# Matmul fillers of 384 columns, fillers between attention and experts, and another order of PSUM banks

## The chip, the cores and the metric

The kernel runs on one core of one Trainium2 chip. A core has TensorE (PE: matmuls, with its weight loads listed apart as PEld), VectorE (DVE), ScalarE (ACT), GpSimd (POOL), and SyncE (SP), which here only issues DMAs. The engines run their own instruction streams and meet at semaphores. PE writes into PSUM[...]; DVE and ACT read PSUM, POOL doesn't touch it here. The metric is device time in microseconds, the median over several executions. One further execution is recorded by the hardware profiler; its rows are what is quoted below.

## The reference: softcapped attention, then soft mixture of experts

Eight batches, twelve heads, 448 tokens, 64 per head. The attention's output, laid out as x of 3584 tokens by 768, is the input of a soft mixture of 8 experts with 4 slots each (32 slots), hidden size 1024.

```python
# attention, per batch and head
scores = cap * np.tanh(scale * (q @ k.T) / cap)          # cap = 30
attn = np.exp(scores - scores.max(-1)); attn /= attn.sum(-1)
x = attn @ v                                             # -> [3584, 768]
# experts
logits = x @ phi                                         # [3584, 32]
d = softmax(logits, axis=0); slot_input = d.T @ x        # [32, 768]
for e in range(8):                                       # 4 slots of each expert
    slot_out[e] = np.maximum(slot_input[e] @ w1[e], 0) @ w2[e]
out = softmax(logits, axis=1) @ slot_out                 # [3584, 768]
```

The slots' sums run over all tokens of all batches. So the experts can't begin before the last token of attention has its logits, and no output can be stored before the experts are done.

## The kernel before: tiling, stages and the order of work

**Attention.** Heads are taken in pairs. A tile is 64 keys of both heads of a pair (two 64x64 corners of the array) against 448 queries. Six tiles make a chunk; there are 56 chunks. For each, `qk_chunk` (L295) writes the scores into PSUM, `tanh_chunk` (L304) and `exp_part` (L308) turn them into bf16 weights on ACT; for some tiles DVE works out the exp by a polynomial (L335 to L340). `pv_mms` (L358) multiplies by the values with a column of ones beside them, `norm` (L365, L368) divides by the row sums into xq, `x_transp` (L406, L411, L417) transposes, `logits` multiplies by phi (L423, L427), and `slot_sums` adds e^logits times x into the slots (L494, L500). The order on each engine is written by hand: `at(j, slot, f, ...)` puts a function into one of the places of chunk j, and `run(j, slot)` plays it there. Nothing is rescheduled, so an instruction that waits holds up all that are queued behind it on its engine.

**Fillers.** `busy(n)` (L612) issues n matmuls of ones by ones, 128 columns each, whose result nobody reads. `spare(n)` gives them a fresh PSUM tile "junk" in the bank that the attention's output uses (pool psV, one buffer); `fill(n)` writes 57 columns beside the output instead. They are placed by the list FILL (10 and 12 in chunk 6 of each batch), by a few calls for the first two chunks, and in the chunks NCH-6, NCH-4 and NCH-2, the last of which has 12. Before the first data arrive, `busy(4)` and `busy(28)` run on a boot tile. The tile of ones is 128x128 and is set by DVE (L77).

**Between attention and experts.** After the last chunk, seven banks of PSUM (b0 to b6) are dealt out by `bank()` from a list, `turns`; when the list is empty it goes on with (6, 3, 0, 1, 2). In order they hold the output of the last pairs (pvm, pvl), the last logits (lpl), the last slot sums (slpl, two banks with 96 columns in use of 512), one half of the last transposes (xpl), the sums of the softmax (zps), then the experts' tiles. The steps on PE are: `x_transp(last - 1)`; `x_last(0)` transposes the first part of the last pair, ACT copies; `z_last(bl - 1)` sums e for the batch before the last; `phi_last(last - 1, ...)`; `x_last(1)`, copied by DVE; `phi_last(last, ...)` for the first two groups of tokens, then `e_last(0)` on ACT; the remaining groups after DVE's copy, then `e_last(1)`; `slot_mms` (L494, L500); DVE adds them to slT (L759); `z_last(bl)`. Then `layer1` (L794): six steps for each of four halves, in every step four matmuls of 512 columns side by side, one per expert, in a quarter of the array's columns each.

**Experts and output.** `relu` on ACT and DVE, `h_transp`, then `layer2` (L827) into two banks so_ps, first for output columns 0 to 383, then for 384 to 767. The first so_ps is copied to so[0] (L878, L879), and while the second half of layer 2 runs, tiles of the output's first half are made by `half_tile` (L858, L863: a matmul by so, a scaling on ACT or DVE, a store from SP). Twelve of these "stored tiles" are made, numbers 0 to 11; number 0 takes two banks, the others one each. The last loop then uses a new pool, `fin`, of three tiles of two banks each in the same memory. A new tile waits until those who used its banks are done. The loop makes first the missing halves of the twelve tiles, still by `half_tile`, then whole tiles (L910, L917, L919). SP issues all stores (L843, L860). The weights w1 and part of w2 come in during attention; the rest of w2 was converted to bf16 in DRAM (w2d) and is read back by SP as w2t from the end of attention on.

Of the kernel before, what the change touches and what calls it, by code (L numbers as in the profile page):

```python
# [9 lines left out]
F32 = mybir.dt.float32  # L10
BF16 = mybir.dt.bfloat16
# [6 lines left out]
P = 128  # L18
# [18 lines left out]
def kernel(  # L37
# [12 lines left out]
    B, H, _, _ = q.shape  # L50
# [3 lines left out]
    NS = moe_phi.shape[1]  # L54
    NJ = D // P
# [13 lines left out]
    pe, dve, act, pool, sp = nc.tensor, nc.vector, nc.scalar, nc.gpsimd, nc.sync  # L69

    consts = ctx.enter_context(tc.tile_pool(name="consts", bufs=1))
# [1 line left out]
    psT = ctx.enter_context(tc.tile_pool(name="psT", bufs=1, space=PSUM))  # L73


    ones = consts.tile([P, P], BF16, name="ones")
    dve.memset(ones, 1.0)  # L77
    ident = consts.tile([P, P], BF16, name="ident")
    make_identity(nc, ident)
# [3 lines left out]
    half1 = consts.tile([P, 1], BF16, name="half1")  # L83
    pool.memset(half1, 0.0)
    pool.memset(half1[0:HP, :], 1.0)
    phib = consts.tile([P, NJ, NS], BF16, name="phib")
    ET4 = consts.tile([P, B // 2 - 1, NT, 2, HP], BF16, name="ET4")
    winv = consts.tile([P, B // 2, NT], F32, name="winv")
# [51 lines left out]
    for nm in ("ex1", "ex2", "vb0", "ex3", "ex4", "ex0", "vb1"):  # L140
        home = exps if nm[0] == "e" else vb
# [4 lines left out]
    psV = attp.enter_context(tc.tile_pool(name="psV", bufs=1, space=PSUM))  # L146
# [65 lines left out]
    def first_pieces(h, jobs):  # L212

        for stage, nm, c0, c1, eng, bank, at0 in jobs:
            copy = act.copy if eng is act else dve.tensor_copy
            cols = slice(h * HP, h * HP + HP)
            if stage == "cast":
                copy(casts[nm, 0][:, c0:c1, cols],
                     raws[nm, 0][h][:, c0 * DH:c1 * DH].rearrange("p (c d) -> p c d", d=DH))
            elif stage == "turn":  # L220
                for c in range(c0, c1):
                    pe.transpose(bank[cols, at0 + c - c0, :], casts[nm, 0][:, c, cols], ident)
            else:
                copy(qkT[nm, 0][cols, c0:c1, :], bank[cols, at0:at0 + c1 - c0, :])
# [146 lines left out]
    def xq_tile(pr):  # L371
        Q, h = divmod(pr, 2)
        if h == 0:
            xq[Q] = xs.tile([P, 2, NT, DH], BF16, name="xq", tag="xq")
# [25 lines left out]
    def turn_x(ps, q0, pr, gs):  # L400

        Q, h = divmod(pr, 2)
        for g in gs:
            c0 = g * P - q0
            if g < NF:
                pe.transpose(ps[:, c0:c0 + P],  # L406
                             xq[Q][:, h, 2 * g:2 * g + 2, :].rearrange("p i d -> p (i d)"), ident)
                continue
            for n in range(2):
                r = slice(n * HP, n * HP + HP)  # L410
                pe.transpose(ps[r, c0:c0 + HP], xq[Q][r, h, NT - 1, :], ident[r, r])  # L411
# [8 lines left out]
    def phi_mms(dst, t, g, jt, first, last):  # L420

        if g < NF:
            pe.matmul(dst, t[:, g * P:(g + 1) * P], phib[:, jt, :], start=first, stop=last,  # L423
                      skip_group_check=True)
            return
        for n in range(2):
            pe.matmul(dst[n * HP:n * HP + HP], t[:, TAIL:S], phib[:, jt, :], start=first,  # L427
                      stop=last, skip_group_check=True)
# [22 lines left out]
    def e_rep(b):  # L451

        e4s[b] = consts.tile([P, NG, 4 * NS], BF16, name="e4", tag="e4", bufs=1)
        pool.tensor_copy(e4s[b].rearrange("p g (a s) -> p g a s", a=4),  # L454
                         es[b].unsqueeze(2).to_broadcast([P, NG, 4, NS]))
# [63 lines left out]
    def at(j, slot, f, *a):  # L519
        if j < 0:  # L520
            j, slot = 0, "b"
        aux.setdefault((j, slot), []).append((f, a))
# [3 lines left out]
        hpads.append(consts.tile([P, E, NFT, NS], BF16, name="hpad", tag="work", bufs=1))  # L526
        pool.memset(hpads[0], 0.0)

    def spare(n):

        busy(n, psV.tile([P, P], F32, name="junk", tag="pv"))

    FILL = ((3, "a", fill, 2), (4, "a", fill, 2), (5, "a", fill, 2), (6, "a", spare, 10), (6, "c", spare, 12), (7, "a", fill, 18), (8, "a", fill, 8), (9, "a", fill, 2))
    PER = 2 * NQB * NT // CH
    assert PER == 7 and NQB == 3
# [11 lines left out]
    for b in range(B):  # L547
        j, p = b * PER, 6 * b
# [10 lines left out]
        if b == 0:  # L559
            at(j + 1, "d", spare, 34)  # L560
            at(j + 2, "d", spare, 4)
# [20 lines left out]
    for n, job in enumerate(wjobs):  # L582
        at(1 + n * (NCH - 5) // len(wjobs), "b", *job)
    for j, slot, n in ((0, "a", 10), (0, "c", 10), (1, "b", 10), (1, "c", 8)):
        at(j, slot, spare, n)
    for j, slot, n in ((NCH - 6, "d", 8), (NCH - 4, "d", 8), (NCH - 2, "d", 12)):
        at(j, slot, spare, n)
    id32s = []
# [18 lines left out]
    junk = boots[0][:, 0, 0:P]  # L607

    def busy(n, home=None, by=None):
        by = ones if by is None else by  # L610
        for _ in range(n):
            pe.matmul(junk if home is None else home, by, by, start=True, stop=True)  # L612

    busy(4, by=nc.const_aps.tensor(1.0, [P, P], BF16))
    junk = boots[1][:, 0, 0:P]
    busy(28)
    first_half(0)
    qk_chunk(0)
# [46 lines left out]
    attp.close()  # L665
    mid = ExitStack()
    big = mid.enter_context(tc.tile_pool(name="big", bufs=1, space=PSUM, reuse_waits="tile"))
    turns = [0, 1, 2, 6, 3, 4, 5, 0, 6, 3, 0, 1, 2, 4, 5]

    def bank(shape, dt=F32, name="bank"):  # L670
        n = turns.pop(0)
        if not turns:
            turns.extend((6, 3, 0, 1, 2))
        return big.tile(shape, dt, name=name, tag=f"b{n}")

    pvs[last - 1] = bank([P, NT, W], name="pvm")
    lps = [bank([P, 2, NS], name="lpl") for _ in range(2)]
    pv2 = [bank([P, 4, W], name="pvl") for _ in range(2)]
    sl_ps = [bank([P, NJ // 2, NS], name="slpl") for _ in range(2)]
    xq_tile(last - 1)  # L680
    run(NCH - 1, "t0")
    CM = sum(place[last - 1, c] < NTILE - 2 * CH for c in range(NT))
# [7 lines left out]
    for s in range(2):  # L690
        pe.matmul(lps[s], id32s[0], lg[:, 2 * s:2 * s + 2, :], start=True, stop=False,
                  skip_group_check=True)
# [12 lines left out]
    def phi_last(pr, gs, done=False):  # L705
        for g in gs:
            phi_mms(lps[g // 2][:, g % 2, :], xTs[pr], g, pr % NJ, False, done)
# [21 lines left out]
    def z_last(b):  # L729
        for g in range(NG):  # L730
            for a in range(4):
                pe.matmul(zl[32 * a:32 * a + NS, :], es[b][:, g, :],
                          ones[:, 0:1] if g < NF else half1, start=(b < bl and g == 0),
                          stop=(b == bl and g == NG - 1), skip_group_check=True)

    def x_last(s, copy):
        q0, q1 = 2 * s * P, min(2 * s * P + 2 * P, S)
        turn_x(xpl[s], q0, last, halves[s])
        copy(xTs[last][:, q0:q1], xpl[s][:, 0:q1 - q0])

    def e_last(s):
        act.activation(el[:, 2 * s:2 * s + 2, :], lps[s], ACT.Exp)

    x_last(0, act.copy)
    z_last(bl - 1)
    phi_last(last - 1, (0, 1, 2))
    x_last(1, dve.tensor_copy)
    phi_last(last, (0, 1), True)
    e_last(0)
    phi_last(last, (2,))  # L750
    phi_last(last - 1, (NF,))
# [7 lines left out]
        dve.tensor_tensor(slT[:, js, :], sl_ps[s], slacc[:, js, :], op=ALU.add)  # L759
    e_rep(bl)  # L760
    z_last(bl)
    dve.tensor_tensor(zacc, zl, zacc, op=ALU.add)
    dve.reciprocal(rz, zacc)
    att.close()
# [131 lines left out]
    for n in range(B // 2 * NT):  # L896
# [12 lines left out]
        for half in range(2):  # L909
            pe.matmul(op[:, half, 0:HD], et_tile(bb, c), so[half],  # L910
                      start=True, stop=True)
# [47 lines left out]
```

## Time and profile before

| what | value |
|---|---|
| median of 4 executions | 303.35 us |
| the four | 303.18, 301.55, 303.59, 303.53 us |
| the profiled execution, its own time | 303.18 us |
| its span, first to last instruction | 301.4 us |
| PE busy, matmuls | 265.2 us (88%), 4687 |
| ACT busy | 268.0 us (89%) |
| DVE busy | 236.8 us (79%) |
| POOL busy | 136.7 us (45%) |
| matmuls of the fillers in junk (L612), 128 columns | 264, 18.9 us busy |
| first matmul of layer 1 | 259.23 us |
| first store issued | 270.76 us |
| last DVE work | about 292.3 us |
| mean granted clock of TensorE | 0.98 |

Busy time of PE counts overlapping matmuls once; a matmul's duration (0.22 us for 128 columns) includes its passage through the array, and in a row of them one starts every 0.056 us. "PEclk" is the share of TensorE's full clock that was granted. In rows of time, `[0.76 <-DVE obh L865]` means that the engine was idle for 0.76 us and that what ended it was DVE's instruction of line 865; "issue" means that the profile shows nothing that it waited for. A row with x3 merges three instructions: its time runs from the first's start to the last's end.

### The profile page before, as it was taken

To read this page: it belongs to the slowest core of one execution; us is meant where nothing else is said; L and a number is where in the kernel's file an instruction comes from. 1 tells how busy PE (TensorE), PEld (TensorE's weight loads), DVE (VectorE), ACT (ScalarE), POOL (GpSimd) and SP (SyncE) were. 2 spreads that over 40 slices of the span, in tenths; PEclk is the share of its full clock that TensorE was granted. 3 is DMA by queue.
4 is the path that set the end of the run, shared out by engine and by line. 5 is a ranking of instruction groups with operands and counts; after the bars stand their busy time and mean duration, and the time that the engine had idled before them with its cause. 6 is when DMAs were issued, how large, how long until landed. Compare 5 with 4: busy or idle time off the path is not lost.

```text
span 301.4 us, 10675 instructions
## 1 busy us (share of the span) xinstructions
PE 265.2 (88%) x4687; PEld 181.4 (60%) x4687; DVE 236.8 (79%) x511; ACT 268.0 (89%) x211; POOL 136.7 (45%) x178
## 2 busy tenths in 40 slices
PE   8898988998899989988999899899999999998830
PEld 6665656665666666666666566666666677542410
DVE  3728989898988999899879998999899973236850
ACT  3999999999999999999999999999999998136740
POOL 4493663485439534953394349443933232000000
PEclk9999999999999999999999999999999999799995
DMA  7999999699999999999899999999999649918997
GB/s 266 199 204 206 206 218 198 141 213 206 232 182 198 200 232 201 208 203 232 152 156 221 229 225 189 195 231 228 171 203 232 194 113 358 410 71 320 403 424 315
DMA packets 58061, 67.70 MB, mean 225 GB/s; under 512 B 3872, under 2 KB 54304, under 8 KB 58016
## 3 DMA queue, kind: packets, MB, share of 16 engines
q0 software_dynamic: 42448, 35.31, 75.8%
q1 hardware_dynamic: 15280, 31.50, 29.1%
q8 instruction: 36, 0.59, 0.7%
q10 hardware_dynamic: 288, 0.23, 0.2%
q14 instruction: 9, 0.07, 0.1%
HBM read 91.32 MB, written 18.87 MB: 366 GB/s over the span
## 4 chain that ended last, share of the span: by engine, by line
ACT 69%; PE 18%; issue 5%; DVE 4%; POOL 1%; DVEq 0%; ACTq 0%
ACT ex L304 37%; ACT ex L308 28%; PE pv L358 3%; PE hp L794 2%; PE so_ps L827 2%; PE sc L295 2%; PE op L910 2%; ACT E L448 1%; ACT ob L919 1%; PE boot L612 1%; PE op L863 1%; DVE xq L368 1%; PE pvl L358 1%; DVE obh L865 1%; POOL vbd L273 1%
## 5 line engine op out<-in xcount | busy, mean ns | idle before, releaser
L304 ACT ACTIVATE ex<-sc 128x1344 bf16<-128x1344 f32 (+1 forms) x113 | 164.3, 1726 | 1.4 <-PE sc L295 1.4
L308 ACT ACTIVATE ex<-ex 128x2240 bf16<-128x2240 bf16 (+4 forms) x58 | 147.1, 2573 | 0.1
L358 PE MATMUL pv<-vbd,ex 128*128 128x130 bf16 (+1 forms) x1610 | 94.4, 211 | 10.4 <-POOL vbd L273 5.4
L358 PEld LDWEIGHTS <-ex 128*128 128x128 bf16 (+1 forms) x1680 | 76.0, 101 | 31.1 <-issue 6.6
L295 PE MATMUL sc<-qT,kT 64*64 64x448 bf16 x672 | 68.8, 359 | 4.7 <-ACT ex L304 3.5
L273 POOL CAST vbd<-vraw 64x896 bf16<-64x896 f32 x23 | 21.9, 952 | 66.3 <-PE pv L358 44.1
L454 POOL COPY e<-E 128x512 bf16<-128x512 bf16 x9 | 5.6, 618 | 64.3 <-ACT E L448 33.0
L339 DVE SCALAR_TENSOR_TENSOR work<-work 128x448 f32<-128x448 f32 x45 | 32.9, 732 | 0.8
L295 PEld LDWEIGHTS <-kT 64*64 64x64 bf16 x672 | 24.7, 105 | 11.4 <-issue 7.6
L338 DVE SCALAR_TENSOR_TENSOR work<-work 128x448 f32<-128x448 uint16 x45 | 31.6, 702 | 0.0
L368 DVE TENSOR_TENSOR xq<-pv,rec 128x448 bf16<-128x448 f32 x46 | 28.7, 624 | 1.6
L340 DVE SCALAR_TENSOR_TENSOR ex<-work 128x448 bf16<-128x448 f32 x45 | 29.3, 651 | 0.7
L274 POOL CAST vbd<-vraw 64x896 bf16<-64x896 f32 x23 | 24.6, 1070 | 1.4
L113 POOL DMA_DIRECT2D w1b<-in_moe_w_dram x32 | 24.6, 771 | 0.0
L417 DVE COPY xT<-xps 128x448 bf16<-128x448 bf16 x46 | 17.9, 388 | 6.9 <-PE xps L411 6.2
L612 PEld LDWEIGHTS <-ones 128*128 128x128 bf16 x292 | 17.9, 102 | 6.4 <-issue 4.3
L335 DVE TENSOR_SCALAR work<-ex 128x448 int32<-128x448 bf16 x45 | 20.6, 457 | 0.0
L612 PE MATMUL junk<-ones 128*128 128x128 bf16 x264 | 18.9, 220 | 1.2 <-DVE xq L368 0.8
L265 DVE COPY kT<-kps 128x896 bf16<-128x896 bf16 x23 | 14.3, 622 | 6.8 <-PE kps L263 6.2
L185 POOL DMA_DIRECT2D kb<-in_k_dram x22 | 16.1, 732 | 6.1 <-PE kps L263 5.8
L337 DVE TENSOR_SCALAR work<-work 128x448 uint16<-128x448 uint16 x45 | 18.4, 409 | 0.5
L185 POOL DMA_DIRECT2D qb<-in_q_dram x22 | 16.2, 735 | 3.3 <-DMA kraw<-in_k_dram 3.3
(129 smaller groups left out, 338.8 us busy)
## 6 DMA issues: line engine op xcount, KB each, us to landing
w1b<-in_moe_w_dram POOLq DMA_DIRECT2D x32, 384.0 KB, 8.6
vraw<-in_v_dram SPq DMA_DIRECT2D x23, 448.0 KB, 5.2
w2d<-in_moe_w_dram POOLq DMA_DIRECT2D x20, 384.0 KB, 9.0
w2t<-w2d SPq DMA_DIRECT2D x20, 384.0 KB, 5.8
out_dram<-ob SPq DMA_DIRECT2D x7, 768.0 KB, 6.4
qb<-in_q_dram POOLq DMA_DIRECT2D x22, 224.0 KB, 8.7
kb<-in_k_dram POOLq DMA_DIRECT2D x22, 224.0 KB, 8.0
w2b<-in_moe_w_dram POOLq DMA_DIRECT2D x12, 384.0 KB, 8.7
```

Of the source, the lines that this page charges most:

```text
L113: pool.dma_start(out=w1b[e][:, js, fs], in_=w1r[:, e, js, fs])
L185: (sp if nm == "v" else pool).dma_start(out=t, in_=quad_ap(nm, Q))
L273: pool.tensor_copy(t[0:HP, :, :, 0:DH], raw[0:HP])
L295: pe.matmul(sc[cs, u, 0:S], qkT["k", Q][r, c, cs], qkT["q", Q][r, :, cs], start=True, stop=True)
L304: act.activation(exs[j][:, half * CS + u0:half * CS + u1, :], sc[:, u0:u1, 0:S], ACT.Tanh, scale=qk_scale / cap)
L308: act.activation(exs[j][:, u0:u1, :], exs[j][:, u0:u1, :], ACT.Exp, scale=cap)
L338: lambda: dve.scalar_tensor_tensor(xp, frac, p2, frac, ALU.add, ALU.mult),
L339: lambda: dve.scalar_tensor_tensor(xp, xp, p1, frac, ALU.add, ALU.mult),
L340: lambda: dve.scalar_tensor_tensor(t, xp, p0, xb, ALU.add, ALU.mult))
L358: pe.matmul(out_, exs[j][r, u, q0:q0 + (HP if tail else P)], v_, start=(c == 0 and g == gs[0] < NF), stop=(c == NT - 1), skip_group_check= ...
L368: dve.tensor_tensor(xq[Q][:, h, s0:s1, :], pv[:, 0:s1 - s0, 0:DH], rec.to_broadcast([P, s1 - s0, DH]), op=ALU.mult)
L612: pe.matmul(junk if home is None else home, by, by, start=True, stop=True)
```

## The change

It has three parts.

*Wider fillers.* The tile of ones becomes 128x384; columns 0 to 127 are set by DVE as before, the rest by POOL. `busy` issues n // 3 matmuls of 384 columns and n % 3 of 128 where its target has more than 128 columns. `spare` makes such a target unless it is told otherwise; the calls of the first two chunks outside the list for batch 0 keep 128.

*New fillers.* In the unused columns of the second slpl bank: `busy(1)` before `x_last(0)`, `busy(3)` after `z_last(bl - 1)`, `busy(6)` after the first `phi_last(last, ...)`. After `z_last(bl)`, twelve matmuls of 128 columns, in turn in the four quarters of the array's columns, in a bank of their own.

*Banks.* `turns` has one entry more, for that bank, and another order behind it.

```diff
-    ones = consts.tile([P, P], BF16, name="ones")
+    wide = consts.tile([P, 3 * P], BF16, name="ones")
+    ones = wide[:, 0:P]
     dve.memset(ones, 1.0)
...
     pool.memset(half1[0:HP, :], 1.0)
+    pool.memset(wide[:, P:3 * P], 1.0)
...
-    def spare(n):
+    def spare(n, parts=3):
-        busy(n, psV.tile([P, P], F32, name="junk", tag="pv"))
+        busy(n, psV.tile([P, parts * P], F32, name="junk", tag="pv"))
...
     for j, slot, n in ((0, "a", 10), (0, "c", 10), (1, "b", 10), (1, "c", 8)):
-        at(j, slot, spare, n)
+        at(j, slot, spare, n, 1)
...
     def busy(n, home=None, by=None):
-        by = ones if by is None else by
+        home, by = junk if home is None else home, ones if by is None else by
+        if home.shape[-1] > P:
+            for _ in range(n // 3):
+                pe.matmul(home, ones, wide, start=True, stop=True)
+            n, home = n % 3, home[:, 0:P]
         for _ in range(n):
-            pe.matmul(junk if home is None else home, by, by, start=True, stop=True)
+            pe.matmul(home, by, by, start=True, stop=True)
...
-    turns = [0, 1, 2, 6, 3, 4, 5, 0, 6, 3, 0, 1, 2, 4, 5]
+    turns = [0, 1, 2, 6, 3, 4, 5, 0, 6, 3, 0, 1, 2, 3, 4, 5]
...
-            turns.extend((6, 3, 0, 1, 2))
+            turns.extend((3, 2, 6, 0, 1))
...
-    sl_ps = [bank([P, NJ // 2, NS], name="slpl") for _ in range(2)]
+    sl_ps = [bank([P, 512], name="slpl") for _ in range(2)]
+    junk = sl_ps[1][:, P:512]
+    sl_ps = [x[:, 0:NJ // 2 * NS].rearrange("p (j s) -> p j s", s=NS) for x in sl_ps]
...
+    busy(1)
     x_last(0, act.copy)
     z_last(bl - 1)
+    busy(3)
     phi_last(last - 1, (0, 1, 2))
     x_last(1, dve.tensor_copy)
     phi_last(last, (0, 1), True)
+    busy(6)
     e_last(0)
...
     z_last(bl)
+    junk = bank([P, P], name="junk")
+    for n in range(12):
+        a = n % 4 * NS
+        pe.matmul(junk[a:a + NS, :], ones[:, 0:NS], ones, start=True, stop=True,
+                  skip_group_check=True)
```

## The prediction, made before the changed kernel was run

> **What bounds the kernel now.** I read the slices of the span first, then stretches of a few microseconds around the end of attention, then the rows in order of time.
>
> ```profile
> PE   8898988998899989988999899899999999998830
> ACT  3999999999999999999999999999999998136740
> PEclk9999999999999999999999999999999999799995
> DMA  7999999699999999999899999999999649918997
> ```
>
> Each digit is one fortieth of 301.4 us, 7.5 us. Three stages follow each other. Up to about 255 us ACT works without a gap (30.00 us busy in every 30 us from 30 to 240 us), so nothing that PE does there counts while it stays ahead of ACT. Then PE carries the time: ACT has next to nothing to do in slices 35 and 36, and there the granted clock falls to 7 tenths. From about 272 us the stores of the output fill the DMA engines to the end. A microsecond won in the second stage starts the stores earlier; it reaches the end if the third stage has nothing else to wait for.
>
> The low digit of the clock is one block of 3.41 us, cut out here with its neighbours and a later stretch of the same length (columns: busy us of PE, weight load, DVE, ACT, POOL, then granted clock, DMA share, GB/s):
>
> ```profile
> 255.38:258.79 3.41, 3.05 (x73) 2.20 (x71) 1.31 (x5) 1.25 (x4) 0.40 (x1) 1.00 1.02 402
> 258.79:262.21 3.42, 3.41 (x60) 1.40 (x58) 0.69 (x4) 0.00 (x0) 0.21 (x1) 0.50 1.03 408
> 262.21:265.62 3.41, 3.41 (x68) 1.61 (x64) 1.04 (x2) 1.37 (x2) 0.00 (x0) 1.00 0.84 335
> 275.86:279.27 3.41, 2.08 (x10) 0.77 (x8) 2.73 (x6) 2.23 (x4) 0.00 (x0) 1.00 0.87 326
> ```
>
> The clock is full, then exactly half for 3.41 us, then full. What lies in the half block is the first layer of the experts (L794), on the path with no cover:
>
> ```profile
> 259.23 5.51 PE L794 MATMUL hp<-w1b,slT 128*32 128x512 bf16 x72
> ...
> 260.49 0.16 PEld L794 LDWEIGHTS <-slT 128*32 128x32 bf16 x4 [0.27 <-issue]
> 260.92 0.16 PEld L794 LDWEIGHTS <-slT 128*32 128x32 bf16 x4 [0.27 <-issue]
> ...
> 262.20 2.06 PEld L794 LDWEIGHTS <-slT 128*32 128x32 bf16 x40 [0.27 <-issue]
> ```
>
> A round is four matmuls side by side. In the block a round begins every 0.43 us (260.49, 260.92); after 262.20 ten rounds pass in 2.16 us, 0.216 each. Seven rounds fill 259.23 to 262.20, 2.97 us, where 7 x 0.216 = 1.51 would do: **the half clock costs 1.46 us**.
>
> **Why it falls, and whether the fillers stop it.** I count the work given to the array: columns streamed, times the share of its 128 x 128 places in use. Matmuls of 384 columns back to back start 0.161 us apart (L863 at 276.81, three of them), so 3.41 us holds some 8,110 full columns. Listed by shape, 255.38 to 258.79 has 18 slot matmuls of 32 columns (576), six of 32 (192), six transposes of 128 (768), three of 130 (390), and small or quarter-array ones (some 310): 2,240, or 2,040 without those that began before it. That is a quarter, and half clock followed. The stretch from 275.86 has ten of 384, eight begun inside it: 3,070, 38%, and the clock stayed. PE's busy share says the opposite (0.89 and 0.61), so the bound must be on columns, somewhere between 2,040 and 3,070.
>
> The new fillers add one of 128, one of 384 and two of 384 columns inside this stretch: 1,280. 2,040 + 1,280 = 3,320, above the stretch that kept its clock. Blocks follow each other from the first clock event at 6.2 us on, and another execution may cut elsewhere: the worst cut I find (from 255.6) has about 1,800, and 3,080 with fillers, just at the mark. The margin is thin, but I take the dip as gone. The four times fit: 303.18, 303.53 and 303.59 against 301.55, a gap of 1.6 to 2.0 us, as if one execution in four had been cut so that it had no dip.
>
> A rule speaks against this part. The Trainium skill (TensorE: Matmul & The Clock Gate, "Why this matters for your kernels") wants no PE-idle gaps over about 3 us and halves the clock after an idle window. Here PE had no gap above 0.21 us and the clock fell. By the rule these fillers can do nothing, and the sum is their price, +0.1; by the rows it is -1.46 + 0.1. I follow the rows.
>
> **Part by part**, against the profiled execution: 303.18 us, of which 301.4 is span and 1.8 lies around it.
>
> *Fillers between attention and experts.* busy(1) goes in at 256.1, where PE waits until 256.38 for DVE's xq: free. busy(3) comes after z_last (last issue 256.69) and before phi_last at 256.90, which waits for ACT's xT copy to 256.84: 0.16 us in a hole of 0.20; with a change of tile shape (such changes cost up to 0.15 us between starts, 256.44 to 256.59) up to 0.07 us late, and behind it wait the last transposes, DVE's copy and the last logits: +0.06. busy(6), 2 x 0.161 = 0.32, starts at 257.34, and the next matmul waits for DVE's xT until 257.70: 0.36 free, +0.02. The twelve of 128 columns go four abreast, 3 x 0.056 = 0.17 us, between 259.07 and layer 1 at 259.23, which waits for slT to 259.18: +0.03. Sum +0.1; without cover they would cost 0.7, at half clock 0.3 or more after their holes.
>
> *After the dip.* Layer 1 ends 1.46 earlier; relu, layer 2 and the first output tiles follow on PE with hardly a gap. The next in line is the reload of w2 (w2t<-w2d), whose transfers end at about 265.2; layer 2 first reads w2t at 267.68, and at 266.2 then. Covered. The stores begin 1.46 earlier and run at the rate they have now.
>
> *Banks.* Today the first tile of the last loop (L910's loop, first with half_tile) takes the two banks of which one held stored tile 11, the very last:
>
> ```profile
> 276.15 0.61 DVE L865 TENSOR_SCALAR obh<-op,winv 128x384 f32<-128x384 f32 x1
> 276.81 0.65 PE L863 MATMUL op<-so,ET 128*128 128x384 bf16 x3 [0.76 <-DVE obh L865]
> 277.18 1.14 DVE L865 TENSOR_SCALAR obh<-op,winv 128x384 f32<-128x384 f32 x2 [0.41 <-PE op L863]
> ```
>
> PE waits 0.76 us for tile 11, and DVE 0.41 for PE. By the new list the first pair's banks held tiles 7 and 8 (evicted by 275.2), and tile 11 sits in the second pair. The first matmul then waits for so[1] alone (DVE L889, 275.68 + 0.56 = 276.24); DVE goes on at 276.76 rather than 277.18, and the store queue, which waits for that tile at 277.4 to 277.8, issues 0.42 earlier. Next to be late are tiles 1 and 2 of the loop, still behind tile 11: they start as today, so between 0 and -0.42. DMA has room there (0.87 from 275.86) and is full later, so I take -0.4 and keep 0 for the range. In the other half-tiles a bank comes round after five in both lists, and the experts' banks were read long before: nothing.
>
> *Merged fillers.* The trace has 264 matmuls junk<-ones; 38 stay narrow, 226 become 84 (142 matmuls and 142 weight loads go). Three narrow ones take 3 x 0.056 = 0.167 us, a wide one 0.161. Two microseconds of PE time at most, behind an ACT without a gap: 0. In the last stretch of attention the chain does run over PE: 12 fillers at 247.33, 0.02 us shorter, then 255.0 as the end of ACT's last exp: 0. In the first 10 us likewise: six fillers at 7.58 become two.
>
> *The wider tile of ones.* One more POOL memset of 128 x 256 (128 x 128 took 0.20 us) at about 1.7; POOL's next work is at 5.0. The boot fillers read columns 0 to 127 and need not wait for it if waits go by region: the first score matmuls start at 6.24, before the last copy into the same kT tile (6.42). If they did wait, +0.8. I take 0.
>
> Sum: -1.46 + 0.1 - 0.4 = -1.76, so 301.4 beside the profiled 303.18; the median of 303.35 lies 0.17 higher, 301.6 from there. **Forecast 301.5 us.**
>
> **Rivals.**
> *The dip stays* or falls elsewhere in layer 1 (the array's count works otherwise, or the margin is too thin). Then the twelve and the wide fillers run partly at half clock, +0.3, and the banks give -0.4: 303.1 (302.7 to 303.5). For it: the thin margin. Against: the stretch at 275.86.
> *The gain is lost in the tail*: the stores are bound by something that does not start earlier, and half of it returns: 302.3. For it: DMA at 1.05 from 279 on. Against: DMA is idle at 268 to 271, waiting for the first tile.
> *Merging lowers the clock in attention*: the count is of starts or weight loads, not columns, and blocks that rest on fillers fall below the bound. PE is busy in nine tenths there, so 3.41 us at half clock puts it some 1.5 us behind, of which ACT feels 0.5 to 1; with one block in each of seven batches, +3.5 to +7: 305 to 308.7. It decides the sign from about three such blocks. Against: ten wide matmuls kept the clock at 275.86; the leanest attention stretch I find holds 40% by columns.
>
> **Chances.** Forecast 0.70 (own range 300.9 to 302.1), dip stays 0.13, lost in the tail 0.09, clock in attention 0.08. A change under 0.5% (1.5 us, so above 301.83) can't be told from none. Of the forecast's 0.70, 0.60 lies below that; the dip that stays, the tail and the rest make 0.32 the same; 0.08 slower. The range, 300.9 to 303.2, takes in most of the second case.
>
> **What would show it.** Right: granted clock 1.00 in every stretch from 250 to 290; layer 1's 18 rounds in 3.9 us; PE's wait before the first L863 of the last loop gone from 0.76 to under 0.3; stores beginning near 269.4. Wrong: a block of 0.50 after 258, one in attention with ACT waiting for sc (L295), or stores that begin earlier and end as before.

## The result and the profile after

The changed kernel takes 301.56 us (median of 43 executions, 301.03 to 303.6) against 303.0 us before (64 executions, 301.24 to 304.69). The ratio is 0.9963, 95% interval 0.9951 to 0.9975: 1.1 us less, between 0.8 and 1.5. The medians differ by more, 1.44 us, for a reason that comes below.

The profiled execution took 301.29 us with a span of 299.5 us. From its page, in the same forty slices:

```profile
PEclk9999999999999999999999999999999999999985
DMA  7999999699999999999899999999999749938997
```

The low digit at the experts is gone; the 8 and the 5 at the end lie behind PE's last work. Stretches of 3.41 us around layer 1, which begins at 258.72 (columns as before: busy us of PE, weight load, DVE, ACT, POOL; granted clock, DMA share, GB/s):

```profile
252.93:256.34 3.41, 3.41 (x67) 2.53 (x66) 1.57 (x5) 2.12 (x5) 0.00 (x0) 1.00 1.00 394
256.34:259.75 3.41, 3.41 (x94) 2.39 (x97) 0.91 (x5) 0.65 (x3) 0.61 (x1) 1.00 1.03 407
259.75:263.16 3.41, 3.41 (x64) 1.40 (x53) 0.75 (x1) 0.69 (x1) 0.00 (x0) 1.00 1.03 409
```

The clock is full in all three. (One profile can't show that the fillers did it: that of only_twelve below, which lacks the wide ones, has no half block there either. The counts below show it.) The place where PE stood 0.76 us for stored tile 11, in the rows in order of time of the changed kernel:

```profile
274.53 1.66 DVE L881 TENSOR_SCALAR obh<-op,winv 128x384 f32<-128x384 f32 x3
...
274.68 0.86 PE L879 MATMUL op<-so,ET 128*128 128x384 bf16 x3 [0.24 <-DVE so L905]
```

PE waits 0.24 us, and for so[1] (DVE, L905), not for a tile. DVE makes three tiles without a pause.

What the two profiles differ by, milestone by milestone (us from the start of the span):

| milestone | before | after | earlier by |
|---|---|---|---|
| clock first full | 6.21 | 3.76 | 2.45 |
| ACT's last exp of attention ends | 255.00 | 254.45 | 0.55 |
| layer 1 begins | 259.23 | 258.72 | 0.51 |
| first transpose of hidden values (behind layer 1's 18 rounds) | 264.68 | 263.06 | 1.62 |
| so[1] ready | 276.24 | 274.62 | 1.62 |
| first store of 768 KB issued | 283.74 | 281.86 | 1.88 |
| last store's transfer ends | 299.87 | 297.98 | 1.89 |

So the 1.9 us of this pair are 0.55 from the start, which is chance (the clock opened earlier against the program), 1.11 in layer 1, 0.26 at the banks, and -0.04 for the fillers. Layer 1 gave 1.46 and lost 0.35 again, to a stop that was not there before. The weight loads of the changed kernel show it:

```profile
258.72 2.93 PEld L810 LDWEIGHTS <-slT 128*32 128x32 bf16 x60
262.11 0.53 PEld L810 LDWEIGHTS <-slT 128*32 128x32 bf16 x12 [0.46 <-issue]
```

After 60 of 72 loads PE stops for a moment, and the row names nothing that it waits for; the cause comes below, with the code fetches. The break falls inside a round of four matmuls (three of the round start at 261.75, the fourth at 262.11), so the last rounds run out of step and one more start is needed.

### The profile page after: what moved, and what is told of

It is laid out like the page before. It is cut to its first block, busy times and chain, and to the rows that moved or that the text cites. A ratio compares the mean times of both kernels' runs of the same rounds, so it can differ in the third digit from the quotient of the medians.

```text
span 299.5 us, 10423 instructions
## 1 busy us (share of the span) xinstructions
PE 263.0 (88%) x4561; PEld 174.7 (58%) x4561; DVE 235.8 (79%) x511; ACT 268.0 (89%) x211; POOL 137.7 (46%) x179
## 4 chain that ended last, share of the span: by engine, by line
ACT 73%; PE 16%; issue 5%; DVE 2%; DMA 1%; POOL 0%; DVEq 0%; SPq 0%; ACTq 0%
ACT ex L306 40%; ACT ex L310 30%; PE pv L360 2%; PE so_ps L843 2%; PE hp L810 2%; PE sc L297 1%; ACT E L450 1%; ACT ob L935 1%; PE op L879 1%; PE boot L618 1%; PE op L926 1%; PE pvl L360 1%; DMA out_dram<-obh 1%; DVE obh L881 1%; PE pvm L360 1%
## 5 line engine op out<-in xcount | busy, mean ns | idle before, releaser
L306 ACT ACTIVATE ex<-sc 128x1344 bf16<-128x1344 f32 (+1 forms) x113 | 161.2, 1673 | 1.2 <-PE sc L297 1.2
L310 ACT ACTIVATE ex<-ex 128x2240 bf16<-128x2240 bf16 (+4 forms) x58 | 143.8, 2509 | 0.1
L340 DVE SCALAR_TENSOR_TENSOR work<-work 128x448 f32<-128x448 uint16 x45 | 30.9, 687 | 0.0
L342 DVE SCALAR_TENSOR_TENSOR ex<-work 128x448 bf16<-128x448 f32 x45 | 30.1, 670 | 0.7
L337 DVE TENSOR_SCALAR work<-ex 128x448 int32<-128x448 bf16 x45 | 19.9, 442 | 0.0
L367 DVE RECIPROCAL rec<-pv 128x7 f32<-128x7 f32 x46 | 9.3, 203 | 9.9 <-PE pv L360 9.5
L408 PE MATMUL xps<-ident,xq 128*128 128x128 bf16 x141 | 15.5, 219 | 1.4 <-DVE slacc L511 1.3
```

What stands on the lines that cost most here:

```text
L306: act.activation(exs[j][:, half * CS + u0:half * CS + u1, :], sc[:, u0:u1, 0:S], ACT.Tanh, scale=qk_scale / cap)
L310: act.activation(exs[j][:, u0:u1, :], exs[j][:, u0:u1, :], ACT.Exp, scale=cap)
L340: lambda: dve.scalar_tensor_tensor(xp, frac, p2, frac, ALU.add, ALU.mult),
L342: lambda: dve.scalar_tensor_tensor(t, xp, p0, xb, ALU.add, ALU.mult))
```

## The experiments

Each execution comes with its span and its mean granted clock. One block of 3.41 us at half clock takes 1.71 / 300 = 0.006 off the mean. Executions without such a block before the stores end lie at 0.984 to 0.989, those with one at 0.983 or less (the tail, where PE is idle, is in all of them). That gives a count beside the ratio. The line is thin: outside the two kernels with a dash, the four executions at exactly 0.983 (one of the changed kernel, two of no_twelve, one of no_twelve_wider) are only 0.3 to 0.4 us longer than the median without a block and may have none. "PE" counts matmuls and weight loads in PE's program (the pages list four more in every kernel, 2 x 4687 = 9374 for before, which changes no difference); "span" is the median span of the executions without a half-clock block. In the two kernels marked with a dash the tail is longer and blurs the count.

| kernel | ratio to before (95%) | with half-clock block | span | PE |
|---|---|---|---|---|
| before, on each of three chips | 1 | 24 of 43, 35 of 45, 17 of 35 | 299.8, 299.65, 299.65 | 9370 |
| changed kernel | 0.9963 (0.9951 to 0.9975) | 5 of 44 | 299.7 | 9118 |
| fill_only | 1.0067 (1.0043 to 1.0091) | - | 301.6 at least | 9402 |
| bank_only | 0.9990 (0.9969 to 1.0011) | 12 of 22 | 299.5 | 9370 |
| merge_only | 1.0012 (0.9992 to 1.0032) | 8 of 22 | 300.3 | 9086 |
| fill_aligned | 0.9982 (0.9963 to 1.0002) | 4 of 22 | 299.9 | 9370 |
| after_44_rows | 1.0012 (0.9992 to 1.0032) | - | 300.6 at least | 9162 |
| no_twelve | 0.9952 (0.9933 to 0.9971) | 3 of 16 | 299.5 | 9118 |
| thin_fillers | 1.0013 (0.9989 to 1.0038) | 8 of 12 | 299.6 | 9118 |
| only_twelve | 1.0001 (0.9967 to 1.0034) | 6 of 12 | 299.45 | 9118 |
| after_again | 0.9981 (0.9959 to 1.0003) | 1 of 12 | 299.6 | 9118 |
| no_twelve_wider | 0.9975 (0.9946 to 1.0003) | 2 of 12 | 299.65 | 9118 |

The kernel before had the block in between half and four fifths of its executions, chip by chip. fill_only, bank_only and merge_only ran on the first chip, fill_aligned, after_44_rows and no_twelve on the second, the last four on the third. Ratios from different chips therefore stand on different ground, and the counts and spans are the surer guide.

### The three parts alone: fill_only, bank_only, merge_only

fill_only takes back merging and the bank order of the stored tiles:

```diff
-    def spare(n, parts=3):
+    def spare(n, parts=1):
-    turns = [0, 1, 2, 6, 3, 4, 5, 0, 6, 3, 0, 1, 2, 3, 4, 5]
+    turns = [0, 1, 2, 6, 3, 4, 5, 0, 6, 0, 3, 0, 1, 2, 4, 5]
-            turns.extend((3, 2, 6, 0, 1))
+            turns.extend((6, 3, 0, 1, 2))
```

> The new fillers alone: attention's fillers stay at 128 columns and the banks of the stored tiles keep their old order. Theory (the array's columns in a 3.41 us block decide the clock, and the fillers lift them over the bound): a half-clock block in layer 1 goes from some three executions in four to one in ten or fewer, layer 1 takes 3.9 us from its first matmul to the last of round 18 in the profile, and the ratio to before is about 0.9965. Rival (the fillers are only a price, the gain comes from the banks or from merging): half-clock blocks as often as before, ratio 1.000 to 1.001.

In the profile the clock is full and layer 1 takes 4.09 us to the transposes (5.45 before), as the theory has it. And yet the kernel is slower, 1.0067: neither theory foresaw it. In its profile so[1] is ready 1.31 us earlier than before and the first 768 KB store goes out 1.31 us earlier, but the last transfer ends 0.35 us later. The end of its DMA work, in stretches of fill_only (the last two columns are the mean busy share of the 16 engines and GB/s):

```profile
288.00:297.00 9.00, 0.81 (x4) 0.29 (x3) 1.94 (x2) 1.21 (x2) 0.00 (x0) 0.78 1.02 424
297.00:298.00 1.00, 0.00 (x0) 0.00 (x0) 0.00 (x0) 0.00 (x0) 0.00 (x0) 0.50 1.00 409
298.00:299.00 1.00, 0.00 (x0) 0.00 (x0) 0.00 (x0) 0.00 (x0) 0.00 (x0) 0.50 0.27 108
299.00:300.00 1.00, 0.00 (x0) 0.00 (x0) 0.00 (x0) 0.00 (x0) 0.00 (x0) 0.50 0.07 28
```

A share of 0.07 is about one engine of sixteen, and from 298.6 on the packets follow each other one at a time: the others are done and one still works. What held it up stands in the page, under the DMA queues (packets, MB, share), and in the packets' times. The pages of before, after and fill_only, in this order:

```profile
q8 instruction: 36, 0.59, 0.7%
q8 instruction: 35, 0.57, 0.7%
q8 instruction: 37, 0.61, 0.7%
```

They are packets of 16,384 bytes, code for PE, one per about 256 instructions of its program. The last two or three of each profile, in us (start, duration), with the first and last issue of a store:

```
before       264.8 0.92   269.6 0.96                 stores 270.8 to 292.3
after        264.0 0.95   268.0 1.33                 stores 269.1 to 290.3
fill_only    264.4 0.88   267.9 1.05   285.9 0.93    stores 269.5 to 291.9
merge_only   264.3 0.88   271.1 1.52                 stores 270.5 to 292.5
```

In fill_only the 37th fetch goes out in the midst of the stores, which keep the engines full. The store that SP issues at 286.09 took 1.87 us to issue; the later ones take 1.12 to 1.22.

bank_only has the new order and nothing else:

```diff
-    turns = [0, 1, 2, 6, 3, 4, 5, 0, 6, 3, 0, 1, 2, 4, 5]
+    turns = [0, 1, 2, 6, 3, 4, 5, 0, 6, 0, 1, 2, 3, 4, 5]
-            turns.extend((6, 3, 0, 1, 2))
+            turns.extend((3, 2, 6, 0, 1))
```

> The new bank order of the stored tiles alone, no new fillers, no merging. Theory: PE's wait before the first matmul of the last loop falls from 0.76 us to under 0.3, the store queue has no wait at that place, the span is 0.3 us shorter at the same clock; dips of the clock as often as before; ratio about 0.999. Rival (the banks carry the change): ratio 0.996 to 0.997. Rival (DMA hides it): ratio 1.000.

From so[1] ready to the first 768 KB store pass 7.23 us instead of 7.50: 0.27 us, and the median span without a half-clock block is 0.3 shorter than before's on that chip. The ratio's interval holds 1, so by timing alone it is not shown. The clock falls as often as before.

merge_only leaves out the new fillers and keeps the old banks:

```diff
-    busy(1)
-    busy(3)
-    busy(6)
-    junk = bank([P, P], name="junk")
-    for n in range(12):
...
-    turns = [0, 1, 2, 6, 3, 4, 5, 0, 6, 3, 0, 1, 2, 3, 4, 5]
+    turns = [0, 1, 2, 6, 3, 4, 5, 0, 6, 3, 0, 1, 2, 4, 5]
```

> Merging of attention's fillers to 384 columns alone, no new fillers, old banks. Theory: same columns, ACT has no gap in attention, so nothing: ratio 1.000 within 0.001, dips as often as before. Rival (the gate counts starts or weight loads): half-clock blocks inside attention in the profile and in the mean clock, 2 us or more slower. Rival (fewer instructions are worth something themselves): 0.998 or lower.

Its profile has no half-clock block in attention, so the first rival is out; nor is it faster, so the second is too. Executions without a block are 0.5 us longer than before's, and the profile shows a fetch in the way again. Its 35th packet starts at 271.1, between the first stores. SP's rows of merge_only at that place:

```profile
270.93 0.38 SPq L868 DMA_DIRECT2D out_dram<-obh  x1
271.41 1.57 SPq L851 DMA_DIRECT2D out_dram<-obh  x1
```

A store whose counterpart in before is issued in 0.37 us took 1.57, and from so[1] to the first 768 KB store pass 8.13 us instead of 7.50.

### The place of the code fetch: fill_aligned, after_44_rows

If that is right, the number of PE's instructions decides the tail, wherever ahead of it they stand. fill_aligned takes 32 of them out of fill_only, in early attention:

```diff
-            at(j + 1, "d", spare, 34)
+            at(j + 1, "d", spare, 18)
```

> The new fillers alone as in fill_only, but 16 fillers of 128 columns fewer in the second chunk of attention, so that PE's program has 9370 instructions as before (fill_only had 9402, the changed kernel 9118). Theory (PE's code comes in blocks of 16 KB, 256 instructions, and 32 more put one fetch among the stores, on one of the 16 DMA engines): no code fetch after the first store, the last store is issued some 8.6 us after the first 768 KB store as before (9.4 in fill_only), ratio 0.996 to 0.998. Rival (the new fillers themselves slow the tail, or their bank does): still 1.005 or more.

The cost is gone: 0.9982, and spans from 299.4. No fetch falls among the stores (the last is at 268.1, the first store at 269.3). Its tail in stretches:

```profile
288.00:297.00 9.00, 0.81 (x4) 0.29 (x3) 1.94 (x2) 1.03 (x2) 0.00 (x0) 0.69 1.02 426
297.00:298.00 1.00, 0.00 (x0) 0.00 (x0) 0.00 (x0) 0.00 (x0) 0.00 (x0) 0.50 0.94 378
298.00:299.00 1.00, 0.00 (x0) 0.00 (x0) 0.00 (x0) 0.00 (x0) 0.00 (x0) 0.50 0.06 22
```

The engines end nearly together. Three of the four executions with a block have a mean clock of 0.970, two or three blocks each; no profile holds one of them, so where these lie is open. after_44_rows is the opposite, the changed kernel with 44 instructions more and the same columns:

```diff
-            at(j + 1, "d", spare, 34)
+            at(j + 1, "d", spare, 34, 1)
```

> The changed kernel with one merged call of early attention (34 fillers) put back to 128 columns: same columns for the array, 44 PE instructions more, 250 us before the end. Theory (place of the code fetch): a fetch of 16 KB among the stores, one DMA engine behind the others at the end, 1 to 2 us slower than the changed kernel: ratio to before 1.000 to 1.003. Rival (merging is worth what its saved PE time is): no more than 0.1 us from the changed kernel, ratio 0.996.

It is slower than the changed kernel, 1.0012. A fetch starts at 286.4, among the stores. The clearest number is the time from the first 768 KB store's issue to the end of the last transfer: 16.13 us before, 16.12 after, 16.13 in fill_aligned, and 17.79 in fill_only as in after_44_rows. **A fetch in that place costs 1.66 us.** Why it costs more than the packet's own 0.93 us is open.

The Trainium skill (Runtime: NRT & Kernel Launch, "Instruction fetch mechanics") says that code streams in blocks of 16 KiB, 256 instructions, on the engine's own DMA queue, and that crossing a block is mostly hidden. Size and distance agree with the packets here. "Mostly hidden" fits most of the 34 to 36 fetches before the stores; where every DMA engine is full and the end waits for the last of them, it does not hold.

It does not hold in layer 1 either: **the stop there is, by all that the profiles show, PE waiting for code.** Six profiles with a full clock have one, mostly shorter than in the changed kernel. It lies behind 8,617 weight loads and matmuls in after, after_again, no_twelve and only_twelve, and behind 8,873, exactly 256 more, in fill_only and fill_aligned, which moves it from load 60 of layer 1 to loads 46 and 62. The rows of fill_only, to be set beside those of the changed kernel above:

```profile
259.28 2.27 PEld L810 LDWEIGHTS <-slT 128*32 128x32 bf16 x46
261.75 1.19 PEld L810 LDWEIGHTS <-slT 128*32 128x32 bf16 x26 [0.20 <-issue]
```

PE goes on 2.19 to 2.41 us after the start of the last fetch packet. after_44_rows, where 44 instructions more ahead move the place, gets there 2.60 us after its packet and no_twelve_wider 2.72, and neither stops; with fetches and places 256 instructions apart paired in order, no other of the 414 pairs in the twelve profiles is under 2.5 us. This is read from the profiles; no run was made to test it.

### What the clock goes by: no_twelve, thin_fillers, only_twelve, no_twelve_wider

no_twelve is the changed kernel without the loop of twelve and its bank, with 24 instructions put back in early attention so that the fetches stay where they were:

```diff
-    junk = bank([P, P], name="junk")
-    for n in range(12):
...
-            at(j + 1, "d", spare, 34)
-            at(j + 2, "d", spare, 4)
+            at(j + 1, "d", spare, 16, 1)
+            at(j + 1, "d", spare, 18)
+            at(j + 2, "d", spare, 4, 1)
```

> The changed kernel without the twelve fillers behind the last slot sums; 24 instructions are put back in early attention (unmerged fillers), so that PE's program keeps 9118. Theory (the wide fillers before the sums carry it): half-clock blocks in at most two executions in ten, layer 1 starts some 0.05 us earlier, ratio 0.996 to 0.997. Rival (the twelve are what tips the gate): half-clock blocks in half of the executions or more, ratio 0.998 or above.

Three executions of 16 with a block at most, and the lowest ratio of all, on the chip where before had most blocks. The twelve do nothing that can be seen.

thin_fillers keeps all 16 new instructions and makes each 8 columns wide (the results of fillers are never read; thin(n) issues n such matmuls of ones):

```diff
-    busy(1)
+    thin(1)
-    busy(3)
+    thin(1)
-    busy(6)
+    thin(2)
-        pe.matmul(junk[a:a + NS, :], ones[:, 0:NS], ones, start=True, stop=True,
+        pe.matmul(junk[a:a + NS, 0:8], ones[:, 0:NS], ones[:, 0:8], start=True, stop=True,
```

> The changed kernel with the same 16 new filler instructions between attention and experts, each of 8 columns instead of 128 or 384 (9118 PE instructions as in the changed kernel). Theory (columns times the share of the array decide the clock): the block before layer 1 holds about a quarter to a third of full work again, the half-clock block returns in more than half of the executions, ratio 0.998 to 1.000. Rival (it is enough that PE is kept busy with instructions, so starts or gaps count): clock stays full, ratio 0.995 to 0.997 as for the changed kernel.

The block is back in 8 of 12 executions and the gain is gone (ratio 1.0013, a little above the expected 0.998 to 1.000). Its profile, the stretch before layer 1 and the next:

```profile
254.62:258.03 3.41, 3.24 (x65) 2.32 (x62) 1.31 (x5) 1.36 (x5) 0.00 (x0) 1.00 1.02 395
258.03:261.44 3.41, 3.41 (x82) 1.99 (x83) 0.71 (x4) 0.18 (x1) 0.61 (x1) 0.50 1.03 408
```

PE is busy 95% of the first stretch and the clock falls. So it is columns that count, not instructions in flight or PE's recorded busy time.

only_twelve drops busy(1), busy(3) and busy(6) and keeps the twelve (8 instructions put back):

```diff
-    busy(1)
-    busy(3)
-    busy(6)
...
-            at(j + 1, "d", spare, 34)
+            at(j + 1, "d", spare, 6, 1)
+            at(j + 1, "d", spare, 28)
```

> The changed kernel without busy(1), busy(3) and busy(6), only the twelve are left (8 instructions put back in early attention, so 9118 again). Theory: the twelve add 384 full columns, 0.047 of a block, and lie at its end; half-clock blocks in about half of the executions or more, ratio 0.997 to 0.999. Rival (the twelve tip the gate): ratio 0.995 to 0.996.

A block in 6 of 12 executions: not much better than without fillers. The ratio, 1.0001, missed the expected 0.997 to 0.999 and is no use here, since 18 of the 35 executions of before on that chip had none either.

after_again is the changed kernel once more, unedited.

> The changed kernel once more, on the chip of the others of this call: 0.995 to 0.997, spans of 299.3 to 300.1 us and a half-clock block in at most one execution in eight.

As expected by span and count. The ratio, 0.9981, missed the expected 0.995 to 0.997; it is nearer to 1 for the reason just given.

no_twelve_wider, an attempt at something better, starts from no_twelve:

```diff
-    busy(1)
+    busy(3)
```

> The changed kernel without the twelve, and with the first filler of 384 columns instead of 128 (it fits before DVE's xq is ready), 9118 PE instructions. Theory: blocks before layer 1 hold 0.4 or more in every cut, no half-clock block there in any execution, nothing added to the path: 0 to 0.1 us below the changed kernel, ratio 0.9945 to 0.9965. Rival (the twelve are needed, or the wider filler delays the transposes): 0.2 us or more above the changed kernel.

It is not told apart from the changed kernel or from no_twelve, and the expectation that no execution would have a block failed: 2 of 12 have one, one of them several (mean clock 0.964). Where they lie, no profile shows.

**One bound for all profiles.** I cut each of the twelve profiles of this study into the clock's blocks of 3.41 us, from the moment when it first opened, and counted columns times the share of the array as in the prediction. Every block that half clock followed held at most 0.31 of full work: 0.25 in before, 0.31, 0.27 and 0.30 in bank_only, merge_only and thin_fillers, at the last pairs; 0.19 or less in the tail. Every block that kept the clock held 0.36 or more. The bound lies between. Columns without the share of the array don't sort the blocks: 0.51 lost the clock (in after_44_rows, the one block that tells the two apart) and 0.38 kept it (before, from 275.86). In fill_only the block from 255.4 held 0.39, where the prediction's sum had 0.41.

Slid in small steps over the last pairs and the steps behind them, a window of 3.41 us also tells how much the cut matters. In before 0.72 of the places hold 0.31 or less (down to 0.20), in thin_fillers 0.75, in only_twelve 0.50; in the seven profiles with the wide fillers no place holds less than 0.36. That fits 76 of 123, 8 of 12 and 6 of 12, but not merge_only, with 0.78 of the places and 8 of 22 executions, so places are perhaps not equally frequent. And it shows how thin the margin is: 0.36 to 0.38 against a bound above 0.31.

One block fell inside attention, in after_44_rows, with 0.29. PE's row there:

```profile
163.50 0.58 PE L265 MATMUL qps<-ident,qb 128*64 128x128 bf16 x14 [2.01 <-DMA qb<-in_q_dram]
```

PE stood two microseconds for a load of q that came late. What is left of half-clock blocks in the changed kernel may well be of this kind; no profile of the changed kernel holds one, so this is not shown.

## Why the prediction was right, and where its sum was off

- *The clock falls for want of columns; 1,280 more stop it.* Shown. Blocks in 5 of 44 executions instead of about two in three, as rare with the wide fillers alone (4 of 22 in fill_aligned, 3 of 16 in no_twelve), back with the same instructions at 8 columns. The rule about idle gaps, weighed in the prediction, would have left these fillers useless.
- *-1.46 for the dip.* The size is right for one execution: layer 1 to the transposes takes 5.45 us with the block, 4.00 in the two profiles with neither block nor stop. The term was mis-sized as a mean: the sum charged every execution with it. The four times shown had one without. The 64 times of before behind the result fall into two heaps, 17 up to 301.75 us and 47 from 302.5 on, whose medians are 1.75 apart; by the clock 5 of 44 have a block after. By estimate (0.73 - 0.11) x 1.75 = 1.1 us, the whole of the measured gain (by the counts on the three chips, 0.62 before, and 1.46 us it would be 0.74; what the heaps differ by beyond layer 1's 1.46 is not traced). The median before lies among the executions with a block and the median after among those without, which is why the medians differ by more, 1.44.
- *Fillers +0.1.* Layer 1 lost 0.04 us of its lead.
- *Banks -0.4.* 0.26 and 0.27 (a bank is one of the tiles of 512 columns that `bank()` deals out). Counted from so[1], the first store of the last loop goes out 0.38 earlier (1.20 us after it instead of 1.58), since SP is still issuing the tile before. In before the two stores behind it followed 0.43 and 0.47 us apart, in after 0.50, so 0.27 is left.
- *Merged fillers: 0.* For time on PE, right. But the step overlooked that every instruction is also code to be fetched. Alone, merging moves a fetch onto the first stores, with executions 0.5 us longer; without it, the new fillers' 32 instructions put a fetch among the last ones and cost 1.66. 284 instructions fewer and 32 more make 252, nearly one block of 256, and the last fetch stays just before the stores (267.96, stores from 269.15). In the changed kernel merging is what makes the fillers pay.
- *Layer 1's 18 rounds in 3.9 us.* Missed: 4.34 to the transposes, and 4.00 at the best. The sum again took PE's code as being there when it is needed. The stop inside layer 1 costs 0.35 and 0.31 us in the two profiles of the changed kernel; four of the six other profiles with a full clock there have it at the same place in a block of code, but layer 1 loses only 0.03 to 0.09 by it, against 4.00 where there is none. It takes back what the banks bring: without a block, spans of the changed kernel (299.7) are those of before (299.65 to 299.8). Why the fetch comes closest to its place in the changed kernel is open.
- *The rivals.* The tail did not swallow the gain (1.62 at so[1], 1.89 at the end), and no profile has a half-clock block that merging made in attention.
- *The number.* That the median, 301.56, came so near the forecast of 301.5 is in part luck. The four executions that it started from had a median of 303.35, 0.35 above that of 64; and the banks' -0.4, which the forecast counts, was spent again in layer 1.

Of the kernels run, no_twelve has the lowest ratio, 0.9952 (0.9933 to 0.9971); its interval overlaps that of the changed kernel, so a gain over it is not shown.

## What to carry to other kernels

Where the granted clock drops to half for 3.41 us, count the columns times the share of the array in the block before it, not PE's busy time; fillers must be wide to be worth anything, and they are free where PE waits for another engine. Count PE's instructions too: find the code queue's packets, and see that none falls where the DMA engines are full and the end waits for them, nor just ahead of a dense run of short instructions on the critical path; a few dozen instructions more or fewer, anywhere ahead, move it. And if something happens in only some executions, take its share from many of them before charging it to the mean.

## What the runs showed of the hardware that was not expected

- A 16 KB fetch of PE's code, among saturating stores, delayed the end by 1.66 us, though the packet itself took 0.93 us; at the first stores SP's issue of one store stretched from 0.37 to 1.57 us.
- In layer 1 PE stood for up to 0.35 us at the same place in a block of 256 instructions, 2.19 to 2.41 us after the start of the code packet ahead of it.
- The clock's blocks begin at another place against the program in every execution: the first full clock came between 3.76 and 6.28 us in the twelve profiles. Between 3.76 and 6.21 attention finished 0.55 us apart.
- Half clock followed a block with PE busy 95% of the time, at 0.30 of full work.
